# A one-token attention and MLP kernel: wq as one row and then seven ahead of K, q in one loop, zero matmuls on TensorE, ScalarE's small loads after a wait

## The chip, the core and the metric

The kernel runs on one core of one Trainium2 chip. The metric is the device time of one execution in microseconds (us), here the median of three runs. The profile is of one further execution, recorded instruction by instruction and packet by packet.

## What is computed

One token `x` (1 x 1024) is normalized to `xn`. One branch is attention over the last 4096 positions of a cache: `q = xn @ wq` gives 32 heads of 128, eight heads share one of four K/V heads, then scores, softmax, `p @ v` and `@ wo`. The other branch normalizes again and runs an MLP with 3584 hidden values. The three are added.

```
xn = layernorm(x)                                   # 1 x 1024
q  = (xn @ wq).reshape(32, 128)                     # wq 1024 x 4096
k, v = last 4096 rows of the caches, 4 heads        # each 4 x 4096 x 128
o  = softmax(q k^T / sqrt(128)) v                   # 8 query heads per K/V head
y  = layernorm(xn)
h  = gelu(y @ w1 + b1)                              # w1 1024 x 3584
out = x + o.reshape(4096) @ wo + h @ w2 + b2        # wo 4096 x 1024, w2 3584 x 1024
```

All inputs are bf16; weights and cache together are some 39.9 MB and each byte is read once.

## The kernel before, in words

**Loads.** SyncE (SP) issues every big load on one queue, q1, in the order of the program: wq rows 0 to 3 of each partition, the K pair 0 (two of the four heads), wq rows 4 to 7, the K pair 1, all of w1 (lines 233 to 237). Then SP waits until VectorE has transposed the last K quarter (`C["kt", 3]`, line 309) and issues V's two pairs into the place of K (L311); then it waits for q and issues w2 in chunks of 16 and 12 rows into the place of wq (L157 again, from line 313); then it waits for the h loop and issues wo in chunks of 16, 11, 4 and 1 rows (L318). A "row" is one row of a weight matrix in each of 128 partitions: 8 KB of wq, 7 KB of w1, 2 KB of w2 and wo. ScalarE issues three small loads at the very start, on queue q10: x, b2 and b1 (lines 168 to 170).

**POOL** builds constants (lines 175 to 220): `QBD` is cleared early, then the identity `identb`, later `GO` is cleared; `C["consts"]` marks the end. Afterwards POOL passes on loads to TensorE: it waits for a load or a transpose and raises `s_feed`, which loops on TensorE wait for with a register `turn` (lines 406 to 420). In the kernel before, that goes for the two halves of wq, the K pairs, w2 and the first wo chunk.

**VectorE** takes x's statistics once TensorE has spread x over 128 partitions (L426), writes `XZ` (line 274), which holds the normalized x as stationary columns for q, then transposes K in four quarters of 128 x 4096 (`turn_k`, L284): three of them in program order before q's own transpose (L292), the copies of q into `QBD` (L303 on VectorE, L305 on ScalarE) and the fourth quarter. Later come the maximum, the transposed probabilities, the gelu and the attention output.

**TensorE** runs in this order: x's two matmuls; q (64 matmuls of 128 x 512, in two halves of wq); b1's four small matmuls (L446); after ScalarE's copy of q (L290) two matmuls that add x and b2 to the result (L454) and four that set biases for the scores (L457, operands of two rows); 32 score matmuls in two halves, one for each K pair, the second waiting for the fourth K quarter; 56 for the MLP's hidden layer (h); 32 for `p @ v`; 88 in eleven rounds of eight for w2 and the first 16 rows of wo; and the rest of wo in small matmuls, four to a row, of which the last row has its weights loaded ahead (L517) and ends the work (L507). All matmuls written with the helper `add` have line 430. Two copies and one small store (L400, L402) end the program.

Of the kernel before, what the change touches and what calls it, by code (L numbers as in the profile page):

```python
# [18 lines left out]
KC = D // 128  # L19
NQ = HQ * DH  # L20
W1_CHUNKS = [8]
WQ_CHUNKS = [4, 4]
W2_CHUNKS = [16, 12]
WO_CHUNKS = [16, 11, 4, 1]
WO_HEAD = 1
XW = 136
PAIRS = 2
# [24 lines left out]
def bass_parallel_sum__sliding_block_cached__mixer_channel_mlp__decode_kernel(  # L52
# [17 lines left out]
    pe, dve, act, pool, sp = nc.tensor, nc.vector, nc.scalar, nc.gpsimd, nc.sync  # L70

    def sems(name, n):
        return [nc.alloc_semaphore(f"{name}{i}") for i in range(n)]

    s_x, s_b1, s_b2, s_v, s_out = (nc.alloc_semaphore(n) for n in ("s_x", "s_b1", "s_b2", "s_v", "s_out"))
    s_w1 = sems("s_w1", len(W1_CHUNKS))
    s_wq = sems("s_wq", len(WQ_CHUNKS))
    s_k = sems("s_k", PAIRS)
    s_wo = sems("s_wo", len(WO_CHUNKS))
    s_w2 = sems("s_w2", len(W2_CHUNKS))  # L80

    DVE = Track(nc, "S_DVE")
    ACT = Track(nc, "S_ACT")
    POOL = Track(nc, "S_POOL")
    done = {n: nc.alloc_semaphore(f"S_PE_{n}") for n in (
        "x", "h", "hT", "q", "sc", "pv", "tot", "fin")}
    s_feed = nc.alloc_semaphore("S_FEED")

    def sb(name, shape, d):
        return nc.alloc_sbuf_tensor(name, shape, d)  # L90

    f32, bf16 = dt.float32, dt.bfloat16
    identb = sb("identb", [128, 128], bf16)
# [7 lines left out]
    OTHER = sb("OTHER", [2, 128], bf16)  # L101
    ALT = sb("ALT", [2, 512], bf16)
    EDGE = sb("EDGE", [2, 132], bf16)
    XBRP = sb("XBRP", [2, 16 * XP], bf16)
    B1R = sb("B1R", [32, F // 32], bf16)
# [6 lines left out]
    XZ = sb("XZ", [128, KC * XW], bf16)  # L112
    YZ = sb("YZ", [128, 192], bf16)
    QBD = sb("QBD", [128, PAIRS * 512], bf16)
# [16 lines left out]
    GO = sb("GO", [128, ROUNDS * STEP + LEAD + 96], bf16)  # L131
# [6 lines left out]
    WA, W1 = BIG[:, 0:KC * NQ], BIG[:, KC * NQ:KC * NQ + KC * F]  # L138
    W2 = WA[:, 0:FC * D]
    PS = nc.alloc_psum_tensor("PS", [128, 8 * 512], f32)  # L140
    PSb = PS[:, :].bitcast(bf16)

    def bank(n, rows=128, first=0):
        return PS[first:first + rows, n * 512:(n + 1) * 512]

    w1_p = B_w1.rearrange("(p r) n -> p r n", r=KC)
    wq_p = A_wq.rearrange("(p r) n -> p r n", r=KC)
# [5 lines left out]
    C = {}  # L153

    def load_chunks(dst, src, chunks, width, semaphores, c0=0):
        for j, n in enumerate(chunks):
            sp.dma_start(  # L157
                dst[:, c0 * width:(c0 + n) * width].rearrange("p (c n) -> p c n", c=n),
                src[:, c0:c0 + n, :],
            ).then_inc(semaphores[j], 16)  # L160
            c0 += n

    XB = XBRP[:, :].rearrange("p (a n) -> p a n", a=16)[:, :, 0:D // 16]

    def row_load(dst, src, semaphore):
        act.dma_start(dst, src.rearrange("o (a n) -> o a n", a=16)).then_inc(semaphore, 16)

    row_load(XB[0:1], A_x.rearrange("b s n -> (b s) n"), s_x)
    row_load(XB[1:2], B_b2.rearrange("(o n) -> o n", o=1), s_b2)
    act.dma_start(B1R[:, :], B_b1.rearrange("(p c) -> p c", p=32)).then_inc(s_b1, 16)  # L170

    def pool_wait():
        pool.wait_ge(POOL.sem, POOL.cnt)

# [44 lines left out]
    POOL.mark(pool.tensor_tensor(out=HALF[:, :], in0=HALF4[:, 0:2], in1=HALF4[:, 2:4], op=ALU.add))  # L219
    C["consts"] = POOL.cnt  # L220

    act.wait_ge(POOL.sem, C["QBD"])
    ACT.mark(act.activation(out=PS[:, 0:1024], in_=QBD[:, :], func=ACTF.Copy))
    ACT.mark(act.activation(out=bank(7), in_=QBD[:, 0:512], func=ACTF.Copy))
# [2 lines left out]
    def pairs(cache, c):  # L227
        return cache[0, 2 * c:2 * c + 2, SK - W:SK, :].rearrange("g (m i) d -> m g (i d)", m=64)

    def load_k(c):  # L230
        sp.dma_start(KV[:, c * 8192:(c + 1) * 8192], pairs(A_k_cache, c)).then_inc(s_k[c], 16)  # L231

    load_chunks(WA, wq_p, WQ_CHUNKS[:1], NQ, s_wq)
    load_k(0)
    load_chunks(WA, wq_p, WQ_CHUNKS[1:], NQ, s_wq[1:], WQ_CHUNKS[0])
    load_k(1)
    load_chunks(W1, w1_p, W1_CHUNKS, F, s_w1)

# [59 lines left out]
    for b in range(4):  # L298
        for c in range(PAIRS):
            to = QD[32 * b:32 * b + 32, c, :, b, 16 * c:16 * c + 16].rearrange("p e (u j) -> p e u j", j=4)  # L300
# [5 lines left out]
    turn_k(3)  # L306

    V = KV[:, :]
    sp.wait_ge(DVE.sem, C["kt", 3])
    for c in range(PAIRS):  # L310
        sp.dma_start(V[:, c * 8192:(c + 1) * 8192], pairs(A_v_cache, c)).then_inc(s_v, 16)  # L311
    sp.wait_ge(done["q"], 8)
    load_chunks(W2, w2_p, W2_CHUNKS, D, s_w2)
    sp.wait_ge(done["h"], 7)
    c0 = 0
    for j, n in enumerate(WO_CHUNKS):
        first = (FC + c0) * D
# [79 lines left out]
    for engine, track, a in ((act, ACT, 1), (dve, DVE, 0)):  # L397
        engine.wait_ge(done["fin"], 1)
        of, to = PS[64 * a:64 * a + 64, 7 * 512 + 256 * a:7 * 512 + 256 * a + 256], Pb[0:64, 256 * a:256 * a + 256]
# [4 lines left out]


    pool_wait()
    pool.wait_ge(s_wq[0], 16)
    pool.sem_inc(s_feed, 1)
    pool.wait_ge(s_wq[1], 16)
    pool.sem_inc(s_feed, 1)  # L410
    pool.wait_ge(DVE.sem, C["kt", 1])
    pool.sem_inc(s_feed, 1)
    pool.wait_ge(DVE.sem, C["kt", 3])
    pool.sem_inc(s_feed, 1)
    for semaphores, chunks in ((s_w2, W2_CHUNKS), (s_wo, WO_CHUNKS[:WO_HEAD])):
        if semaphores is s_wo:
            pool.wait_ge(ACT.sem, C["OT"])
        for semaphore, n in zip(semaphores, chunks):
            pool.wait_ge(semaphore, 16)
            pool.sem_inc(s_feed, n // ROUND)  # L420
    pe.wait_ge(POOL.sem, C["ones"])
    turn = pe.alloc_register("turn")
    pe.reg_mov(turn, 1)
    pe.wait_ge(s_x, 16)
    for i in range(2):
        last = pe.matmul(bank(2 + i), lhsT=onesb[0:1, :], rhs=XB[0:1, 8 * i:8 * i + 8, :])  # L426
    last.then_inc(done["x"], 1)

    def add(to, lhsT, rhs, **place):
        return pe.matmul(to, lhsT=lhsT, rhs=rhs, start=False, stop=False, skip_group_check=True, **place)  # L430

    pe.wait_ge(DVE.sem, C["xz"])
    with pe.Fori(0, len(WQ_CHUNKS)) as j:
        pe.wait_ge(s_feed, turn)
        pe.reg_add(turn, turn, 1)
        with pe.Fori(0, 4) as t:
            for u in range(2):
                for k in range(4):
                    last = add(bank(7), XZ[:, bass.ds(t * 2 + j * (4 * XW) + (XW * k + u), 128)],
                               WA[:, bass.ds(t * -1024 + j * (4 * NQ) + (k * NQ + (7 - u) * 512), 512)])  # L440
            last.then_inc(done["q"], 1)

    pe.wait_ge(s_b1, 16)
    turned = PS[:, 2 * 512 + 32:2 * 512 + 64].rearrange("p (c t) -> p c t", c=4)[:, :, 0:7]
    for q in range(4):
        pe.matmul(turned, lhsT=E4[:, q * 128:(q + 1) * 128],  # L446
                  rhs=B1R[:, q * FC:(q + 1) * FC].rearrange("p (t c) -> p c t", c=4),
                  start=(q == 0), stop=False, skip_group_check=True)
# [4 lines left out]
    for a in range(2):  # L453
        pe.matmul(bank(7), lhsT=EDGE[:, 1 - a:129 - a], rhs=XB[:, 8 * a:8 * a + 8, :], start=(a == 0), stop=False,  # L454
                  skip_group_check=True)
    for n in range(4):
        pe.matmul(bank(3 + n), lhsT=OTHER[:, :], rhs=ALT[:, :], start=True, stop=False, skip_group_check=True)  # L457
    pe.wait_ge(DVE.sem, C["d_QBD"])
    K4 = KT[:, :].rearrange("p (x k) -> p x k", k=128)
    with pe.Fori(0, PAIRS) as c:  # L460
# [3 lines left out]
        with pe.Fori(0, 2) as j:  # L464
            for n in range(4):
                for u in range(2):
                    last = add(bank(3 + n), QBD[:, bass.ds(c * 512 + j * 256 + u * 128, 128)],
                               K4[:, bass.ds(c * 64 + 16 * n, 16), bass.ds(j * 64 + 32 * u, 32)])
                last.then_inc(done["sc"], 1)

    def h_cols(row, t):
        return row.rearrange("p (m a c) -> p m a c", m=128, a=7)[:, :, bass.ds(t, 1), :]

    pe.wait_ge(s_w1[0], 16)
    with pe.Fori(0, 7) as t:
        for k in range(KC):
            last = add(bank(0), YZ[:, bass.ds(t + 8 * k, 128)], h_cols(W1[:, k * F:(k + 1) * F], t))
# [5 lines left out]
    for c in range(4):  # L483
        last = add(turned[:, c], H8[:, c:512:4], FLIP[:, 0:7])
# [6 lines left out]
    with pe.Fori(0, 8) as i:  # L491
        for u in range(4):
            last = add(bank(1), PT[:, bass.ds(i * 256 + u * 64, 128)], V3[:, :, bass.ds(i * 1024 + u * 256, 256)])
# [12 lines left out]
    def add_held(to, lhsT, rhs, column):  # L506
        return pe.add_instruction(mybir.InstMatmult(  # L507
            name=nc.get_next_instruction_name(), engine=pe.engine, start_tensor_calc=False, stop_tensor_calc=False,
            tile_size=(128, 32), tile_position=(0, column), bass_skip_group_check=True, ldweights=False,
            ins=[pe.lower_ap(rhs), pe.lower_ap(lhsT, for_matmul_weights=True)], outs=[pe.lower_ap(to)]))  # L510

    for j, n in enumerate(WO_CHUNKS[WO_HEAD:]):
        held = c0 + n == 32
# [5 lines left out]
        for c in range(c0, c0 + n):  # L519
            rhs = BIG[:, (FC + c) * D:(FC + c + 1) * D]  # L520
            for a in range(4):
                first, column = LEAD + 2 * (c - TAIL) - (0 if a % 2 else ROW), 7 * 512 + a // 2 * 256
                to, of = PS[32 * a:32 * a + 32, column:column + 256], rhs[:, TAIL_AT[a]:TAIL_AT[a] + 256]
                if held:
                    last = add_held(to, OT[:, first:first + 32], of, 32 * a)
                else:
                    last = add(to, OT[:, first:first + 32], of, tile_position=(0, 32 * a))
# [32 lines left out]
```

## Time and profile before

| what | value |
|---|---|
| three runs, median (lowest, highest) | 98.8 us (98.8, 98.97) |
| the profiled execution | 99.37 us |
| its span, first to last instruction | 97.4 us |
| bytes moved | 39.88 MB, mean 409 GB/s over the span |
| time of q1's packets, share of 16 engines | 95.7% |
| TensorE, VectorE busy | 73.0 us, 38.9 us |
| mean granted TensorE clock | 0.965 |

How to read it: times inside the profile count from the first instruction; 1.97 us of the profiled execution lie outside its span. PE is TensorE's matmuls, PEld its weight loads, DVE VectorE, ACT ScalarE, SP SyncE; a "q" behind an engine's name is its issuing side. In a row of the timeline stand the start, the duration of a merged group, the engine, the line, the operation, what it writes and reads, the count, and in brackets how long the engine had been idle and what ended that. A matmul's record is longer than its share of the engine, as matmuls overlap: the spacing between starts is what counts. DMA engines work on packets; each load here is one packet for each partition, spread over 16 engines.

### The profile page before, as it was taken

The numbers are of one execution on the slowest core, as the hardware profiler recorded it, in microseconds if no ns is written. First come the engines' busy times: TensorE is split into PE (matmuls) and PEld (weight loads), VectorE is DVE, ScalarE is ACT, GpSimd is POOL, SyncE is SP. The second block draws the span as 40 slices with busy tenths as digits, with TensorE's granted clock in tenths as the row PEclk, the third lists the DMA queues.
The fourth block names the chain that finished last, engine by engine and source line by source line (L and its number), as shares of the span: only waits on it lengthen the run. The fifth ranks groups of instructions, "written<-read, shape, count | busy, mean of one in ns | idle before, by whom it ended". The sixth has DMA issues, their size and how long they took to land.

```text
span 97.4 us, 1285 instructions
## 1 busy us (share of the span) xinstructions
PE 73.0 (75%) x354; PEld 30.4 (31%) x354; DVE 38.9 (40%) x54; ACT 11.2 (12%) x20; POOL 9.9 (10%) x27
## 2 busy tenths in 40 slices
PE   0004000099999986999979999799999999779992
PEld 0000000033444431333434444333343443334450
DVE  0002899899930799940293620050048000000001
ACT  0880000600000024000005200200000000000001
POOL 6999400000000000000000000000000000000000
PEclk9999999999999998557999999999999999999999
DMA  7599999999999998888999999999999999899890
GB/s 215 256 431 431 405 432 444 431 444 431 410 431 481 636 424 377 377 377 377 437 431 431 437 498 431 431 444 394 394 464 498 431 431 431 376 435 426 372 377 1
DMA packets 1989, 39.88 MB, mean 409 GB/s; under 512 B 322, under 2 KB 324, under 8 KB 452
## 3 DMA queue, kind: packets, MB, share of 16 engines
q1 hardware_dynamic: 1876, 39.85, 95.7%
q10 hardware_dynamic: 112, 0.01, 0.1%
q8 instruction: 1, 0.02, 0.1%
HBM read 39.86 MB, written 0.00 MB: 409 GB/s over the span
## 4 chain that ended last, share of the span: by engine, by line
DMA 80%; PE 14%; SPq 3%; issue 1%; DVE 0%
DMA BIG<-in_B_w_dram 47%; DMA BIG<-in_A_wo_dram 33%; PE PS L430 13%; SPq L231 1%; SPq L157 1%; SPq L318 1%; DVE Pb L400 0%; PE PS L507 0%
## 5 line engine op out<-in xcount | busy, mean ns | idle before, releaser
L430 PE MATMUL PS<-BIG,XZ 128*128 x64 | 16.5, 427 | 10.2 <-DVE B L277 10.2
L430 PE MATMUL PS<-BIG,GO 128*128 (+1 forms) x148 | 22.2, 337 | 1.4 <-POOLq L420 1.2
L284 DVE STREAM_TRANSPOSE KT<-KV 128x4096 bf16<-128x4096 bf16 x4 | 17.6, 4432 | 4.8 <-DMA KV<-in_A_k_cache_dram 4.8
L430 PEld LDWEIGHTS PS<-BIG,GO 128*128 (+1 forms) x148 | 9.9, 97 | 13.8 <-issue 6.4
L430 PEld LDWEIGHTS PS<-BIG,XZ 128*128 x64 | 6.9, 108 | 20.3 <-issue 14.3
L430 PE MATMUL PS<-BIG,YZ 128*128 x56 | 12.4, 380 | 0.6 <-DMA BIG<-in_B_w_dram 0.6
L430 PE MATMUL PS<-KT,QBD 128*128 x32 | 10.0, 491 | 1.0 <-ACT QBD L305 1.0
L430 PE MATMUL PS<-KV,KT 128*128 x32 | 8.3, 381 | 0.5
L400 DVE CAST Pb<-PS 64x256 bf16<-64x256 f32 x1 | 0.4, 417 | 20.4 <-PE PS L507 20.4
L430 PEld LDWEIGHTS PS<-BIG,YZ 128*128 x56 | 5.4, 96 | 7.6 <-issue 1.8
L426 PE MATMUL PS<-XBRP,onesb 1*128 1x512 bf16 x2 | 1.0, 616 | 8.1 <-DMA XBRP<-in_A_x_dram 8.1
L430 PEld LDWEIGHTS PS<-KT,QBD 128*128 x32 | 3.8, 120 | 7.2 <-issue 5.2
L244 DVE BATCH_NORM_STATS2 BN<-PS 128x6 f32<-128x512 f32 x2 | 1.3, 689 | 9.1 <-PE PS L426 9.1
L430 PEld LDWEIGHTS PS<-KV,KT 128*128 x32 | 3.1, 96 | 5.3 <-issue 3.8
L332 DVE TENSOR_REDUCE MX<-PS 128x1 f32<-128x1024 f32 x2 | 2.4, 1220 | 5.6 <-PE PS L430 5.6
L379 DVE SCALAR_TENSOR_TENSOR QBD<-PS,REC,HALF 32x256 f32<-32x256 f32 x2 | 0.9, 474 | 6.9 <-PE PS L430 6.8
L344 ACT ACTIVATE Pb<-PS,NMB 128x2048 bf16<-128x2048 f32 x1 | 2.0, 1968 | 13.8 <-DVE NMB L341 13.8
L348 DVE STREAM_TRANSPOSE KT<-Pb 128x2048 bf16<-128x2048 bf16 x1 | 2.3, 2311 | 2.1 <-ACT Pb L344 2.1
L353 DVE COPY HT<-PS 128x28 f32<-128x28 f32 x1 | 0.2, 210 | 6.4 <-PE PS L430 6.4
L400 ACT ACTIVATE Pb<-PS 64x256 bf16<-64x256 f32 x1 | 0.4, 381 | 20.1 <-PE PS L507 20.1
L426 PEld LDWEIGHTS PS<-XBRP,onesb 1*128 1x128 bf16 x2 | 0.1, 104 | 8.1 <-DMA XBRP<-in_A_x_dram 8.1
L290 ACT ACTIVATE Pb<-PS 128x512 bf16<-128x512 f32 x1 | 0.6, 597 | 16.6 <-PE PS L430 16.6
(77 smaller groups left out, 37.7 us busy)
## 6 DMA issues: line engine op xcount, KB each, us to landing
BIG<-in_A_wq_dram SPq DMA_DIRECT2D x2, 4096.0 KB, 18.8
BIG<-in_B_w_dram SPq DMA_DIRECT2D x1, 7168.0 KB, 46.0
KV<-in_A_k_cache_dram SPq DMA_DIRECT2D x2, 2048.0 KB, 23.1
KV<-in_A_v_cache_dram SPq DMA_DIRECT2D x2, 2048.0 KB, 13.6
BIG<-in_B_w_dram SPq DMA_DIRECT2D x1, 4096.0 KB, 24.8
BIG<-in_A_wo_dram SPq DMA_DIRECT2D x1, 4096.0 KB, 23.5
BIG<-in_B_w_dram SPq DMA_DIRECT2D x1, 3072.0 KB, 31.4
BIG<-in_A_wo_dram SPq DMA_DIRECT2D x1, 2816.0 KB, 29.8
```

What stands on the lines that cost most here:

```text
L157: sp.dma_start(dst[:, c0 * width:(c0 + n) * width].rearrange("p (c n) -> p c n", c=n), src[:, c0:c0 + n, :],).then_inc(semaphores[j], 16)
L231: sp.dma_start(KV[:, c * 8192:(c + 1) * 8192], pairs(A_k_cache, c)).then_inc(s_k[c], 16)
L244: DVE.mark(dve.bn_stats(out=BN[:, 12 * n + 6 * i:12 * n + 6 * i + 6], in_=src[:, 512 * i:512 * i + 512]))
L284: C["kt", n] = DVE.mark(dve.transpose(KT[:, n * 4096:(n + 1) * 4096], KV[:, n * 4096:(n + 1) * 4096]))
L318: sp.dma_start(BIG[:, first:first + n * D], wo_flat[:, c0 * D:(c0 + n) * D]).then_inc(s_wo[j], 16)
L332: C["mx"] = DVE.mark(dve.tensor_reduce(out=MX2[:, n:n + 1], in_=S[:, 1024 * n:1024 * n + 1024], axis=AX.X, op=ALU.max))
L344: C["exp"] = ACT.mark(act.activation(out=Pb[:, :], in_=S, func=ACTF.Exp, bias=NMB[:, 0:1], scale=SCALE, accum_out=SUMP[:, 0:1]))
L348: C["d_pt"] = DVE.mark(dve.transpose(PT[:, 0:2048], Pb[:, :]))
L379: DVE.mark(dve.scalar_tensor_tensor(out=ONM.rearrange("p (i c d) -> p i c d", i=2, c=PAIRS)[:, i], in0=PS[rows, 512:1024].rearrange("p (c ...
L400: track.mark(act.activation(out=to, in_=of, func=ACTF.Copy) if a else dve.tensor_copy(to, of))
L426: last = pe.matmul(bank(2 + i), lhsT=onesb[0:1, :], rhs=XB[0:1, 8 * i:8 * i + 8, :])
L430: return pe.matmul(to, lhsT=lhsT, rhs=rhs, start=False, stop=False, skip_group_check=True, **place)
```

## The change

It does these things:

- wq is loaded as one row and then seven, both ahead of K (before: four rows, K pair 0, four rows, K pair 1).
- ScalarE waits for `identb` before it issues x, b2 and b1; its clearing of PSUM stands behind them as before.
- TensorE multiplies zeros (`QBD`, 40 matmuls of 128 x 512) into bank 4 after x's matmuls; it then waits for both wq loads itself and runs q in one loop of eight rounds of eight.
- POOL's passing on of wq is gone, and TensorE waits for POOL's constants itself.
- The four bias matmuls for the scores become a loop, each with two matmuls of zeros (`GO`) added into bank 1.
- V's first pair is issued after the second K quarter's transpose, the second pair after the fourth (before: both after the fourth).
- wo's chunks are 16, 10, 5 and 1 rows.

```diff
-WQ_CHUNKS = [4, 4]
+WQ_CHUNKS = [1, 7]
-WO_CHUNKS = [16, 11, 4, 1]
+WO_CHUNKS = [16, 10, 5, 1]
...
-    row_load(XB[0:1], A_x.rearrange("b s n -> (b s) n"), s_x)
-    row_load(XB[1:2], B_b2.rearrange("(o n) -> o n", o=1), s_b2)
-    act.dma_start(B1R[:, :], B_b1.rearrange("(p c) -> p c", p=32)).then_inc(s_b1, 16)
...
+    act.wait_ge(POOL.sem, C["identb"])
+    row_load(XB[0:1], A_x.rearrange("b s n -> (b s) n"), s_x)
+    row_load(XB[1:2], B_b2.rearrange("(o n) -> o n", o=1), s_b2)
+    act.dma_start(B1R[:, :], B_b1.rearrange("(p c) -> p c", p=32)).then_inc(s_b1, 16)
     act.wait_ge(POOL.sem, C["QBD"])
...
-    load_chunks(WA, wq_p, WQ_CHUNKS[:1], NQ, s_wq)
+    load_chunks(WA, wq_p, WQ_CHUNKS, NQ, s_wq)
     load_k(0)
-    load_chunks(WA, wq_p, WQ_CHUNKS[1:], NQ, s_wq[1:], WQ_CHUNKS[0])
     load_k(1)
...
-    sp.wait_ge(DVE.sem, C["kt", 3])
     for c in range(PAIRS):
+        sp.wait_ge(DVE.sem, C["kt", 2 * c + 1])
         sp.dma_start(V[:, c * 8192:(c + 1) * 8192], pairs(A_v_cache, c)).then_inc(s_v, 16)
...
-    pool.wait_ge(s_wq[0], 16)
-    pool.sem_inc(s_feed, 1)
-    pool.wait_ge(s_wq[1], 16)
-    pool.sem_inc(s_feed, 1)
...
-    pe.wait_ge(POOL.sem, C["ones"])
+    pe.wait_ge(POOL.sem, C["QBD"])
...
+    def busy(zeros, to, **how):
+        for i in range(2):
+            pe.matmul(to, lhsT=zeros[:, 0:128], rhs=zeros[:, 0:512], skip_group_check=True, **how)
+
+    with pe.Fori(0, 20):
+        busy(QBD, bank(4), start=True, stop=True)
+    for s in s_wq:
+        pe.wait_ge(s, 16)
     pe.wait_ge(DVE.sem, C["xz"])
-    with pe.Fori(0, len(WQ_CHUNKS)) as j:
-        pe.wait_ge(s_feed, turn)
-        pe.reg_add(turn, turn, 1)
-        with pe.Fori(0, 4) as t:
-            for u in range(2):
-                for k in range(4):
-                    last = add(bank(7), XZ[:, bass.ds(t * 2 + j * (4 * XW) + (XW * k + u), 128)],
-                               WA[:, bass.ds(t * -1024 + j * (4 * NQ) + (k * NQ + (7 - u) * 512), 512)])
-            last.then_inc(done["q"], 1)
-
+    with pe.Fori(0, 8) as t:
+        for k in range(KC):
+            last = add(bank(7), XZ[:, bass.ds(t + XW * k, 128)], WA[:, bass.ds(t * -512 + (k * NQ + 7 * 512), 512)])
+        last.then_inc(done["q"], 1)
+
+    pe.wait_ge(POOL.sem, C["consts"])
     pe.wait_ge(s_b1, 16)
...
-    for n in range(4):
-        pe.matmul(bank(3 + n), lhsT=OTHER[:, :], rhs=ALT[:, :], start=True, stop=False, skip_group_check=True)
+    with pe.Fori(0, 4) as n:
+        pe.matmul(PS[:, bass.ds(n * 512 + 3 * 512, 512)], lhsT=OTHER[:, :], rhs=ALT[:, :], start=True, stop=False,
+                  skip_group_check=True)
+        busy(GO, bank(1), start=False, stop=False)
```

## The prediction, made before the changed kernel was built or run

> **What bounds the kernel now.** I read the DMA lines first, because the kernel is one token of attention and MLP over 39.85 MB of weights and cache.
>
> ```profile
> span 97.4 us, 1285 instructions
> PE 73.0 (75%) x354; PEld 30.4 (31%) x354; DVE 38.9 (40%) x54; ACT 11.2 (12%) x20; POOL 9.9 (10%) x27
> PEclk9999999999999998557999999999999999999999
> q1 hardware_dynamic: 1876, 39.85, 95.7%
> ```
>
> SP's queue q1 carries all big loads and its packets fill 95.7% of 16 engines' time; no compute engine comes near that. The packet records say the same more sharply: from 2.4 us (when the last of 16 engines starts) to 94.3 us an engine always has a packet. The first packets start at 1.83 us, SP having issued at 0.81. In steady state a 32 KB packet takes 1.213 us (432 GB/s over 16 engines); 39.85 MB at that rate is 92.2 us. Span = 1.83 start + 92.2 + about 0.9 (staggered start and slow first packets, below) + 0.4 from the last packet to the last landing (95.36) + 2.05 tail = 97.4.
>
> Second, the order of landings on q1. Issue plus the time in the DMA view gives wq first half 12.9, K0 17.8, wq second half 27.5, K1 32.3, W1 49.25, V 54.1 and 59.0, W2 68.7 and 75.9, wo 85.6, 92.3, 94.72, 95.36: strictly in order of issue. A load's landing depends on the bytes ahead of it, so long as it is issued before the queue runs dry.
>
> Third, the chain and the timeline of the end: how far TensorE is from being the bound.
>
> ```profile
> 83.71 1.03 PE L430 MATMUL PS<-BIG,GO 128*128 x4
> 85.92 9.46 PE L430 MATMUL PS<-BIG,GO 128*128 x92 [1.18 <-POOLq L420]
> 93.23 1.10 PEld L430 LDWEIGHTS PS<-BIG,GO 128*32 128x32 bf16 x44 [0.42 <-issue]
> 94.76 0.34 PEld L430 LDWEIGHTS PS<-BIG,GO 128*32 128x32 bf16 x16 [0.43 <-DMA BIG<-in_A_wo_dram]
> 95.10 0.11 PEld L517 LDWEIGHTS <-GO 128*32 128x32 bf16 x4
> 95.40 0.28 PE L507 MATMUL PS<-BIG,GO 128*32 128x256 bf16 x4
> ```
>
> TensorE idles before 85.92 for the 16-row wo chunk, before 94.76 for the 4-row one and before 95.40 for the last. From the last matmul's start at 84.35 plus one spacing of 0.216 to 85.92 it has about 1.3 us of slack; then 0.4 us before 94.76 (ends about 94.36) and 0.2 before 95.40. From h on it has no other wait of weight, so a delay s of the h loop reaches the end only beyond roughly **1.8 us**: 1.3 + 0.4 + 0.2, less 0.1 for the last weight loads of L517.
>
> Fourth, the middle:
>
> ```profile
> 18.80 8.76 DVE L284 STREAM_TRANSPOSE KT<-KV 128x4096 bf16<-128x4096 bf16 x2
> 32.35 4.45 DVE L284 STREAM_TRANSPOSE KT<-KV 128x4096 bf16<-128x4096 bf16 x1 [4.79 <-DMA KV<-in_A_k_cache_dram]
> 36.72 0.67 DVE L292 STREAM_TRANSPOSE Pb<-Pb 128x512 bf16<-128x512 bf16 x1
> 38.14 4.45 DVE L284 STREAM_TRANSPOSE KT<-KV 128x4096 bf16<-128x4096 bf16 x1
> 38.99 10.04 PE L430 MATMUL PS<-KT,QBD 128*128 x32 [0.96 <-ACT QBD L305]
> 49.61 12.44 PE L430 MATMUL PS<-BIG,YZ 128*128 x56 [0.57 <-DMA BIG<-in_B_w_dram]
> ```
>
> VectorE transposes K0 early, waits 4.79 us for K1, and turns q 4.4 us after that. The scores start at 38.99; their first 14 matmuls stand 0.427 us apart and the rest 0.216, with the granted clock at 0.50 from 38.20 to 45.03. q shows the same two spacings (12 slow ones, to 24.5).
>
> **The change, part by part.**
>
> *wq as 1 + 7 rows, before K.* Packets per engine: 16 x 1.213 = 19.41 us become 8 x 0.309 (the 8 KB packets of wo) + 8 x 2.116 (the 56 KB packets of W1) = 19.40. The stream gains nothing. What moves is landings: wq is whole after 8.39 MB, so at 27.5 - 4.86 (one K pair, 17.81 - 12.94) = 22.6; K0 at 27.5 instead of 17.8; K1 and W1 as before.
>
> *The start.* The first 16 packets took 1.72 to 2.15 us where later ones took 1.213, all but one over 1.7: about 0.58 us lost. The out store's first packet came 0.77 us after its issue, wq's 1.02. If both excesses come from the large first packets or from ScalarE's issues at the same 0.81, the change saves up to 0.8 us; if they are a fixed price of starting, nothing. A smaller packet could also lose, but the 8 KB wo packets ran at 424 GB/s; I bound that at +0.1. The packet that started last (2.43) was the fastest at 1.415 and ended with the others, which looks like one fixed moment before which nothing flows. I take **0**.
>
> *ScalarE's loads* wait for identb (POOL, 2.56 by the timeline), so x is issued near 2.6 instead of 0.81, and ScalarE's zeroing of PSUM and the square root's table load behind them shift by 1.8 us, into idle time. Queue q10 takes turns with q1 packet by packet: x waited for three 32 KB packets, its completion for one more. Between 8 KB packets x would land near 5.7; behind 56 KB ones up to 12. The layernorm takes 10.4 us from x to XZ (8.04 to 18.46), so XZ is there at 16 to 22.4, before wq at 22.6. Free. b2 and b1 follow later, unneeded before 36.
>
> *Zero matmuls ahead of q.* 40 of them after x's two. The slow spacing lasted 5.2 us at q and 6.0 at the scores, and the clock's half stretch 6.83; I allow 3.4 (half of that) to 6.8. So they take 40 x 0.216 + half of that = 10.3 to 12.1 us, and end between 17 and 24. They stand behind x's matmuls and behind a wait on POOL met at 2.0 us; queued behind them is only q, which waits for wq. They cost nothing unless x is late. Then q: 64 x 0.216 = 13.8 us from 22.7, done at **36.5**, or 38 to 40 if the clock has fallen again. Before, 35.9.
>
> *What hides that.* VectorE: kt0, kt1, kt2 run back to back from 27.5, 8.76 + 4.45 - so kt2 ends near **40.6** (before 36.8), and q's transpose stands behind it in program order. So q may be late by 3.5 us for nothing, but everything after kt2 moves by 3.8 us: scores start 42.8, kt3 ends 46.4.
>
> *Zero matmuls ahead of the scores.* Four biases and eight zeros: 12 x 0.216 = 2.6 us, from q's copy at 37.2 to about 40.2, and not in the way of 42.8. GO's zeros and the added wait for POOL's constants (11.0) are met long before.
>
> *Scores and h.* At the full clock the first half ends at 46.3, the second waits for kt3 and ends at 50.1: h is late by s = 0.5. With a slow stretch T from 42.8 it ends at 42.8 + 32 x 0.216 + T/2, so s = 0.15 + T/2: 1.85 for T = 3.4, up to 3.5 for 6.8. The max, exp and P transposes (52.25 to 56.65) shift too, before PV at 63.
>
> *V on two waits.* SP waits kt1 (36.3), then kt3 (46.4); before both went at 42.6. Behind the second wait stand V1 and W2. The queue works on W1 till 48.2 and V0 till 53.1, so V1 issued at 46.4 has 6.7 us to spare. W2 is needed at 58, wo at 75 and issued at 62 + s. Free; it would cost if kt3 came after 52.
>
> *wo as 16, 10, 5, 1.* Bytes and packets are the same (9.16 us per engine both ways); the third chunk still lands at 94.72. Its 20 weight loads take 0.43 instead of 0.34, the last four then end at 95.30, under 95.40. Zero, at most +0.1.
>
> **Sum:** stream 0 (-0.8 to +0.1), TensorE at the end 0 (to +1.7), tail 0 (to +0.1). The profiled execution took 99.37 us, 1.97 around its span; the median shown is 98.8. The sum is zero on either base, so 98.8.
>
> **A rule that speaks on TensorE's slow stretch.** By the trace, full-array matmuls ended at 35.7, only ones of 32 and 2 rows followed, and the half clock came at 38.20; an idle stretch of 1.4 us before 85.92 left the spacing at 0.216. The Trainium skill, "TensorE: Matmul & The Clock Gate", section "Part 1: The HAM clock gate", says a free-running window of some 3.4 us decides, idle ones halving the clock and busy ones restoring it, whichever phase the kernel starts in. The trace agrees: 6.83 is two such windows. By that rule an idle 2.6 us alone need not halve the clock, and the sum would stay 0; by the row, 2.5 us with small matmuls in it did.
>
> **Rivals.**
> - *Faster: the start.* The first packets lose less. For it: 0.58 + 0.25 us of excess right where the change acts. Against: the common end of the first packets. About -0.5: 98.3. Chance 0.28.
> - *Slower: cold scores.* TensorE idles from 40.2 to 42.8 behind kt2, the clock halves, and T of 5.2 to 6.0, as seen, makes s = 2.75 to 3.15; minus 1.8 the end moves by 0.95 to 1.35: **100.0**. It decides from T of about 3.3. For it: the half clock at 38.20 after a like pause. Against: a q that runs late closes the pause, and T = 3.4 costs only 0.05. Chance 0.25.
> - *The zeros do not lift the clock* (no zero operand stands in the trace; the two-row ones did not hold it). Then 40 x 0.427 = 17 us push q to 25, q ends at 41 to 42, the twelve matmuls take 5.1 us, scores start near 47.5 and cold; s near 7, end +5: 104. Chance 0.05.
> - *The stream sets the end as before:* 98.8. Chance 0.42, of which a little falls outside 0.2%.
>
> **The numbers.** A measurement of this kernel can tell about 0.2% (0.2 us) from no change. Faster 0.29, same 0.38, slower 0.33. The range leaves out 104 and the ends of both other rivals: 98.2 to 100.0. The likeliest case alone: 98.6 to 98.95.
>
> **What would show it.** q1 with no empty stretch, wo's landings at the same times within 0.2 us (else the start: look at the first packets' starts and lengths); wq's last landing near 22.6, kt2's end near 40.6, scores from 42.8; the clock row in the 42 to 50 us slices; the idle before the 16-row wo rounds shrunk from 1.18 us but not gone. If that idle is gone and TensorE waits for nothing at the end, the slow rival holds. If q1 runs dry anywhere, I am wrong on V.

## The result and the profile after

The changed kernel takes 99.16 us in the median of ten runs, the kernel before 98.83 in ten beside it: the ratio is 1.0034 (95% interval 1.0021 to 1.0047), 0.33 us slower. Forecast was 98.8, no change within 0.2%. The profiled execution of the changed kernel has a span of 97.65 us against 97.41; the shares outside the spans differ from one profiled execution to the next (1.41 and 1.96 us), so I compare spans and places inside them.

The page of the changed kernel: its first line, the line of busy times, the row of the big loads' queue, and the engines' shares of the chain that ended last. Line numbers move with the edit: L425 is now the helper `add`, L429 the matmuls of zeros, L421 x's two matmuls, L508 the last four and L518 their weight loads.

```profile
span 97.6 us, 1414 instructions
PE 81.0 (83%) x391; PEld 34.0 (35%) x402; DVE 38.9 (40%) x54; ACT 11.2 (11%) x20; POOL 9.9 (10%) x27
...
q1 hardware_dynamic: 1876, 39.85, 95.4%
...
PE 83%; DMA 9%; issue 3%; POOL 2%; ACT 1%; DVE 0%; POOLq 0%
```

The queue is as full as before (95.4% against 95.7%), but the chain has changed owner: DMA had 80% of it before, now TensorE (PE) has 83%. That share does not say that 83% of the time would go if TensorE were faster; it says that from the last matmul back to x's landing TensorE hardly waited. The timeline of TensorE's end shows it:

```profile
82.74 13.06 PE L425 MATMUL PS<-BIG,GO 128*128 x103
...
93.99 1.54 PEld L425 LDWEIGHTS PS<-BIG,GO 128*32 128x32 bf16 x60 [0.42 <-issue]
95.53 0.10 PEld L518 LDWEIGHTS <-GO 128*32 128x32 bf16 x4
95.64 0.28 PE L508 MATMUL PS<-BIG,GO 128*32 128x256 bf16 x4
```

Before, three waits for wo stood here (before 85.92, 94.76 and 95.40). All are gone: the matmuls run in one piece, the 60 small ones of the second and third chunk too, and the last four start at 95.64 because TensorE gets to them then. The last load had landed at 95.44 (95.36 before); the 16-row chunk at 85.62, to the digit as before. TensorE was late, the loads were not. How it became late is in the middle:

```profile
11.65 1.03 PE L421 MATMUL PS<-XBRP,onesb 1*128 1x512 bf16 x2 [11.65 <-DMA XBRP<-in_A_x_dram]
12.62 11.47 PE L429 MATMUL PS<-QBD 128*128 128x512 bf16 x40
23.93 13.98 PE L425 MATMUL PS<-BIG,XZ 128*128 x64
...
42.66 4.08 PE L425 MATMUL PS<-KT,QBD 128*128 x16
47.38 4.12 PE L425 MATMUL PS<-KT,QBD 128*128 x16 [0.64 <-issue]
51.64 12.43 PE L425 MATMUL PS<-BIG,YZ 128*128 x56
```

and in VectorE's rows beside it:

```profile
27.35 13.10 DVE L283 STREAM_TRANSPOSE KT<-KV 128x4096 bf16<-128x4096 bf16 x3 [4.84 <-DMA KV<-in_A_k_cache_dram]
40.38 0.67 DVE L291 STREAM_TRANSPOSE Pb<-Pb 128x512 bf16<-128x512 bf16 x1
41.08 0.68 DVE L302 COPY QBD<-Pb 32x64 bf16<-32x64 bf16 x4
41.79 4.45 DVE L283 STREAM_TRANSPOSE KT<-KV 128x4096 bf16<-128x4096 bf16 x1
```

The three K transposes, q's transpose and the start of the scores stand where the prediction put them (40.4 for 40.6, 42.66 for 42.8), and the clock stayed full. But the two halves of the scores take 4.08 and 4.12 us where 16 records 0.216 us apart span 3.6; the second half starts at 47.38 where 46.6 was expected, with "issue" named as what it waited for (nothing that the profile shows, so TensorE's own issuing side); and h starts at 51.64, so s is 2.03 us, not 0.5.

### The profile page after: what moved, and what is told of

It reads as the page before. It is cut to its first block, busy times and chain, and to the rows that moved or that the text cites. A ratio compares the mean times of both kernels' runs of the same rounds, so it can differ in the third digit from the quotient of the medians.

```text
span 97.6 us, 1414 instructions
## 1 busy us (share of the span) xinstructions
PE 81.0 (83%) x391; PEld 34.0 (35%) x402; DVE 38.9 (40%) x54; ACT 11.2 (11%) x20; POOL 9.9 (10%) x27
## 3 DMA queue, kind: packets, MB, share of 16 engines
q1 hardware_dynamic: 1876, 39.85, 95.4%
## 4 chain that ended last, share of the span: by engine, by line
PE 83%; DMA 9%; issue 3%; POOL 2%; ACT 1%; DVE 0%; POOLq 0%
PE PS L425 66%; PE PS L429 14%; DMA XBRP<-in_A_x_dram 9%; PE PS L456 1%; PE PS L421 1%; POOL QBD L174 1%; ACT Pb L289 1%; PE PS L453 1%; ACT H L349 1%; DVE Pb L399 0%; POOL identb L176 0%; POOL onesb L171 0%; POOL identb L173 0%; PE PS L508 0%; POOLq L176 0%
## 5 line engine op out<-in xcount | busy, mean ns | idle before, releaser
L425 PE MATMUL PS<-BIG,GO 128*128 (+1 forms) x137 | 21.3, 333 | 0.7
L425 PEld LDWEIGHTS PS<-BIG,GO 128*128 (+1 forms) x148 | 10.0, 97 | 12.2 <-issue 5.2
L425 PE MATMUL PS<-BIG,XZ 128*128 x64 | 14.0, 379 | 0.0
L425 PE MATMUL PS<-BIG,YZ 128*128 x56 | 12.4, 379 | 0.1
L429 PE MATMUL PS<-QBD 128*128 128x512 bf16 x40 | 11.5, 459 | 0.0
L421 PE MATMUL PS<-XBRP,onesb 1*128 1x512 bf16 x2 | 1.0, 616 | 11.7 <-DMA XBRP<-in_A_x_dram 11.7
L425 PEld LDWEIGHTS PS<-BIG,XZ 128*128 x64 | 6.3, 98 | 7.5
L425 PE MATMUL PS<-KT,QBD 128*128 x32 | 8.0, 379 | 1.0 <-issue 0.6
L425 PE MATMUL PS<-KV,KT 128*128 x32 | 8.3, 381 | 0.5
L425 PEld LDWEIGHTS PS<-BIG,YZ 128*128 x56 | 5.4, 96 | 7.2 <-issue 1.5
L429 PEld LDWEIGHTS PS<-QBD 128*128 128x128 bf16 x40 | 4.5, 114 | 7.4 <-issue 4.4
L425 PEld LDWEIGHTS PS<-KT,QBD 128*128 x32 | 3.1, 96 | 5.9 <-issue 3.8
L425 PEld LDWEIGHTS PS<-KV,KT 128*128 x32 | 3.1, 96 | 5.3 <-issue 3.7
L421 PEld LDWEIGHTS PS<-XBRP,onesb 1*128 1x128 bf16 x2 | 0.1, 106 | 11.7 <-DMA XBRP<-in_A_x_dram 11.7
```

The source lines that it names most:

```text
L429: pe.matmul(to, lhsT=zeros[:, 0:128], rhs=zeros[:, 0:512], skip_group_check=True, **how)
```

## The experiments

Theory 1: TensorE comes to the h loop 2.0 us late, which is more than the slack of 1.8, and the lateness beyond the forecast's 0.5 arises at the ends of the score loops. Theory 2: the loads, the start of the stream or ScalarE's later loads cost the time, and TensorE's place in the chain is incidental. A name with a_ is an edit of the changed kernel, with b_ of the one before. Every ratio is against runs of the kernel before on the same chip.

One table first, since most runs are read by it. From p @ v on, the work of TensorE is the same in all these kernels (a_h6 leaves work out ahead of it); without a wait the last matmuls start 30.57 us after it, as in the changed kernel (95.64 - 65.07).

| kernel | h starts | p @ v starts | that + 30.57 | last wo landing | last matmuls start | ratio (95% interval) |
|---|---|---|---|---|---|---|
| before | 49.61 | 63.05 | 93.62 | 95.36 | 95.40 | |
| b_wq_134 | 49.74 | 63.17 | 93.74 | 95.50 | 95.55 | 1.0007 (0.9988 to 1.0025) |
| a_h6 | 51.82 | 63.51 | 94.08 | 95.39 | 95.44 | 1.0003 (0.9983 to 1.0023) |
| a_j_unrolled_fit | 50.29 | 63.74 | 94.31 | 95.39 | 95.44 | 1.0007 (0.9986 to 1.0027) |
| b_delay8 | 51.05 | 64.49 | 95.06 | 95.45 | 95.50 | 0.9999 (0.9969 to 1.0028) |
| changed | 51.64 | 65.07 | 95.64 | 95.44 | 95.64 | 1.0034 (1.0021 to 1.0047) |
| a_wo_back | 51.79 | 65.22 | 95.79 | 95.40 | 95.79 | 1.0028 (1.0016 to 1.0041) |
| a_half_zeros | 51.84 | 65.28 | 95.85 | 95.40 | 95.84 | 1.0032 (1.0015 to 1.0048) |
| a_no_score_zeros | 52.06 | 65.50 | 96.07 | 95.28 | 96.07 | 1.0042 (1.0018 to 1.0066) |
| b_delay_loop | 52.08 | 65.52 | 96.09 | 95.45 | 96.05 | 1.0047 (1.0029 to 1.0066) |
| b_k_behind_v_split | 52.09 | 65.53 | 96.10 | 95.59 | 96.09 | 1.0042 (1.0018 to 1.0065) |
| a_loads_first | 52.17 | 65.61 | 96.18 | 95.71 | 96.17 | 1.0069 (1.0044 to 1.0094) |

The last matmuls start, within 0.05 us, at the later of two columns: the last landing (plus 0.05) or p @ v plus 30.57. In the first five rows it is the landing and the time is that of the kernel before; in the others it is TensorE, and every one is slower. The change-over lies at p @ v = 95.40 - 30.57 = 64.83, which is 1.78 us after the 63.05 of the kernel before.

**Is TensorE's lateness the cause?** First a pure delay in the kernel before, eight matmuls of zeros:

```
     pe.wait_ge(s_w1[0], 16)
+    for _ in range(8):
+        add(bank(1), GO[:, 0:128], GO[:, 0:512])
```

> The kernel before with eight zero matmuls (8 x 0.216 = 1.73 us) added on TensorE between the wait for w1 and the h loop: pure delay, by about as much as the changed kernel's. By the prediction's slack of 1.8 us: h starts near 51.3, the rounds of wo's 16 rows move by 0.4, the end by 0 to 0.1: 98.8 to 98.95. If the slack is smaller than read, up to 99.5. Theory 2 expects the delay to cost nothing and the changed kernel to be slow for another reason, so 98.83.

It took 98.88 beside 98.98 (two of its twelve times, 100.11 and 100.61, stand apart): p @ v 1.44 us late, nothing at the end. Then less work in the changed kernel, which leaves out one of the seven rounds of h (a seventh of it, not an eighth) and counts to six in the two waits for them:

```
-    sp.wait_ge(done["h"], 7)
+    sp.wait_ge(done["h"], 6)
...
-    act.wait_ge(done["h"], 7)
+    act.wait_ge(done["h"], 6)
...
-    with pe.Fori(0, 7) as t:
+    with pe.Fori(0, 6) as t:
```

> The changed kernel with six instead of seven rounds of the h loop: an eighth of the MLP's first product is left out, so TensorE has 8 matmuls (1.75 us) less to do after the scores; loads, waits and code stay. Theory 1 (TensorE, 2.0 us late at h against 1.8 of slack, sets the end): TensorE idles again 1.0 to 1.3 us before wo's 16-row rounds, the last matmuls wait for the last load, and the time falls to 98.8 to 98.9. Theory 2 (the loads, the start or ScalarE's later loads cost the 0.33 us): it stays at 99.1 to 99.2.

```profile
85.96 8.59 PE L425 MATMUL PS<-BIG,GO 128*128 x72 [0.78 <-POOLq L415]
94.81 0.73 PE L425 MATMUL PS<-BIG,GO 128*32 128x256 bf16 x20 [0.26 <-DMA BIG<-in_A_wo_dram]
95.44 0.28 PE L508 MATMUL PS<-BIG,GO 128*32 128x256 bf16 x4
```

98.85 beside 98.87, and TensorE waits for wo again. The loads, their order and ScalarE's order were those of the changed kernel, wo's 16 rows landed at 85.67, and the 0.33 us were gone: theory 2 falls. A larger delay in the kernel before, as a loop of three times four zero matmuls at the place of b_delay8:

```
+    with pe.Fori(0, 3):
+        for _ in range(4):
+            add(bank(1), GO[:, 0:128], GO[:, 0:512])
```

> The kernel before with twelve zero matmuls ahead of the h loop as a loop of three times four (13 more instructions of program, less than the sixteen of b_delay8, whose fetch stayed in the tail): h starts 2.7 to 3.0 us late (8 x 1.73 / 8 + loop ends, less the 0.3 that b_delay8 found hidden in the wait for w1). Theory 1, one for one beyond a slack of 1.8 us: last matmul 0.9 to 1.2 later, 99.7 to 100.0, with wo's landings unmoved (85.6, 94.7, 95.4). If b_delay16's 101.0 was TensorE's lateness and not its moved fetch, more than that.

99.45 beside 98.88. h was only 2.47 us late, as the twelve zeros ran through at 0.216 us each (49.49 to 52.08) and their loop's ends cost nothing; the last matmuls are 0.65 late, and 2.47 - 1.78 is 0.69. One for one, as expected.

**Where does the lateness come from?** K's order alone, on the kernel before:

```
-    load_k(0)
     load_chunks(WA, wq_p, WQ_CHUNKS[1:], NQ, s_wq[1:], WQ_CHUNKS[0])
+    load_k(0)
```

> The kernel before with one edit: the first K pair is loaded behind both halves of wq, as in the changed kernel. Theory 1 (the order of K alone makes TensorE late; the zero matmuls only win a part of it back): the second K pair's transpose ends near 40.4, the scores start near 42.7 after a pause of more than 5 us, at half the clock for 3.4 to 6.8 us, h starts 2.5 to 3.2 us later than before, and the time is 99.5 to 100.2, slower than the changed kernel. If instead the zeros, the one q loop or ScalarE's loads are what costs: 98.83.

It took 100.91 beside 98.88 (ratio 1.0196, 1.0172 to 1.0220), above the range: h started at 52.34 as expected, but V's two loads, issued together at 46.35, landed at 56.3 and 61.1 (before: 54.1 and 59.0), and all of w2 and wo came 2.1 us later. That was the loads, not TensorE. With V on two waits (the changed kernel's edit of line 309) the two parts separate:

```
-    load_k(0)
     load_chunks(WA, wq_p, WQ_CHUNKS[1:], NQ, s_wq[1:], WQ_CHUNKS[0])
+    load_k(0)
...
-    sp.wait_ge(DVE.sem, C["kt", 3])
     for c in range(PAIRS):
+        sp.wait_ge(DVE.sem, C["kt", 2 * c + 1])
```

> b_k_behind with V's two loads on two waits, as in the changed kernel: the first at 36.3, the second at 46.4. Theory 1: the queue stays full, wo lands at 85.6 and 95.4 as before, h starts near 52.3 as in b_k_behind (2.7 us late, 0.9 beyond the slack), and the time is 99.6 to 99.9. If K's order cost something besides TensorE's lateness, more; if TensorE's lateness were not what counts, 98.88.

99.43 beside 98.93, wo at its old place, TensorE 2.5 us late. K's order is what makes TensorE late. The same joint wait put back into the changed kernel:

```
+    sp.wait_ge(DVE.sem, C["kt", 3])
     for c in range(PAIRS):
-        sp.wait_ge(DVE.sem, C["kt", 2 * c + 1])
```

> The changed kernel with both loads of V issued after the fourth K transpose, as in the kernel before: at 46.3, some 2 us before the queue's last packets of w1 are served. By b_k_behind, V's first half lands at 56.3 instead of 54.1 and everything behind it 2.1 us later: 100.9 to 101.3. If the short notice was an accident of that kernel: 99.1 to 99.2.

Its four times lie between 99.08 and 102.31, median 101.08; they are too far apart for a ratio. In the profile V landed at 55.9 and 60.8. Four such times give no price by themselves, and one of them is no slower than the changed kernel; the six times of b_k_behind (100.12 to 101.58) carry it. In both profiles V was issued some 2 us before w1's last packets were served and landed 1.8 to 2.2 us late; why is open. In the changed kernel, with the split, V landed at 54.1 and 59.0 as before.

Then the loop ends. The scores of the changed kernel written out in full:

```
-    with pe.Fori(0, PAIRS) as c:
-        pe.wait_ge(s_feed, turn)
+    for c in range(PAIRS):
+        pe.wait_ge(s_feed, 1 + c)
...
-        with pe.Fori(0, 2) as j:
+        for j in range(2):
...
```

> The changed kernel with its score loops written out (same 32 matmuls, constant waits on the same semaphore), so that TensorE's issuing side has no loop ends there. Theory 1 (the changed kernel is late because TensorE reaches the h loop 2.0 us later than before, 1.5 us of it lost at the ends of the score loops and at the start of the second half): h starts near 50.2 to 50.5 instead of 51.64, TensorE idles again before the 16-row rounds of wo (0.3 us or more), and the time falls to 98.8 to 98.9. Theory 2 (the loads or the start cost it, not TensorE): the time stays near 99.16 though h starts earlier. Rival within theory 1 (the fourth K transpose and the hand-over by POOL set the second half, not the loops): h starts at 51.0 or later, 99.0 to 99.1.

TensorE did what theory 1 says, as its timeline shows, and yet the time rose to 100.37 (ratio 1.0137, 1.0108 to 1.0167):

```profile
42.63 3.62 PE L425 MATMUL PS<-KT,QBD 128*128 128x512 bf16 x16
46.49 3.61 PE L425 MATMUL PS<-KT,QBD 128*128 128x512 bf16 x16 [0.24 <-POOLq L409]
49.94 12.44 PE L425 MATMUL PS<-BIG,YZ 128*128 x56
...
87.41 9.71 PE L425 MATMUL PS<-BIG,GO 128*128 x92 [0.70 <-POOLq L415]
96.95 0.28 PE L508 MATMUL PS<-BIG,GO 128*32 128x256 bf16 x4
```

The halves take 3.62 and 3.61 us and h starts at 49.94, 1.70 us earlier. But TensorE waits again for wo, whose 16 rows landed at 86.89 instead of 85.62. The DMA view, cut to 77 to 79 us of this kernel, names an intruder:

```profile
q1 hardware_dynamic: 28, 0.92, 107.7%
q8 instruction: 1, 0.02, 2.9%
```

One 16 KB packet of instructions at 77.77 us, 0.93 us on one engine of the 16. The kernel before has the same packet, at 94.85, when its loads are all but through; the changed kernel at 95.08. The packets of the 16 rows show what it does: fifteen engines end their shares at 84.74 to 85.24 us, as in the changed kernel, and the sixteenth at 86.45. Its packet right behind the instructions also took 1.71 us instead of 1.213, so it lost 0.93 + 0.50 us, and the load landed when it was through. I took the early packet to come from the longer program, and tried the same unrolling on the kernel before, where TensorE has slack to spare:

> The kernel before with its score loops written out: 28 more instructions of TensorE's program ahead of the rounds of w2 and wo. Theory 3 (a longer program moves the 16 KB instruction fetch from the tail at 94.9 us into the middle of wo's load, where one engine serves it while its share of wo waits): the fetch stands near 77 to 80, the landings of wo move by 1.2 to 1.4, the rounds' spacing widens, and the time is 100.1 to 100.4, though TensorE's own work is no later. Rival (written-out scores were slower in the changed kernel for a reason of that kernel): 98.83.

100.15 beside 98.87 (1.0120, 1.0092 to 1.0147), the packet at 80.36, one engine through at 86.62 and the others by 85.50, wo 1.4 us late: so it is. TensorE was later too, against the expectation (p @ v at 64.82, as h began in a half-clock stretch), but 64.82 + 30.57 = 95.39 is still ahead of the last landing at 96.75. b_delay16, twice the delay of b_delay8, had run into the same thing:

```
+    for _ in range(16):
+        add(bank(1), GO[:, 0:128], GO[:, 0:512])
```

> The kernel before with sixteen zero matmuls (3.45 us) at the same place. By the slack of 1.8 us the end moves by 1.65: 100.5. Without any slack 102.3; if TensorE is not near the bound at all, 98.83.

101.0 beside 98.98, but with the packet at 79.13, wo landing 1.4 us late and TensorE's rounds 1.82 to 1.98 us apart, it says nothing on the slack; b_delay_loop has the same kind of delay without the moved packet. For the loop ends a shorter program was needed. Only the inner loop written out, with part of the small matmuls for b1, x and b2 left out to make room (not shown):

```
...
-        with pe.Fori(0, 2) as j:
+        for j in range(2):
```

> The changed kernel with the inner score loop written out (two loop ends less, the outer one stays), and three of b1's four matmuls and one of the two that add x and b2 left out, so that the program ahead of the rounds is 11 instructions longer instead of 18. Theory 1 with the loop ends as the late step: the score halves last 3.6 instead of 4.1 us, h starts 0.6 to 0.8 us earlier (50.8 to 51.0), TensorE is inside its slack of 1.8 us and the time is 98.85 to 98.95, if the instruction fetch stays near 95. If the fetch moves to 77 to 80, 100.1 or more, and the run says nothing on the loop ends' time. If loop ends do not matter, 99.16.

h came to 50.27, but the packet still came at 77.69: 100.2 beside 98.93, and nothing learnt on the time. All six of those matmuls left out:

> The changed kernel with the inner score loop written out and, to keep the program short, b1's four matmuls and the two that add x and b2 left out (their waits stay): the program ahead of the rounds is 7 instructions longer than the changed kernel's. Theory 1 with the loop ends as the late step: h starts near 50.3 (1.3 us earlier than in the changed kernel), p @ v near 63.7 instead of 65.07, TensorE idles again before wo's 16-row rounds, the fetch stays near 95, and the time is 98.85 to 98.95. If it stays at 99.1 to 99.2 with the fetch near 95, lateness at h is not the cause. If the fetch moves again, 100.1 or more.

```profile
42.57 3.61 PE L425 MATMUL PS<-KT,QBD 128*128 x16 [0.28 <-ACT QBD L304]
46.84 3.61 PE L425 MATMUL PS<-KT,QBD 128*128 x16 [0.66 <-POOLq L409]
50.29 12.44 PE L425 MATMUL PS<-BIG,YZ 128*128 x56
...
86.20 1.67 PE L425 MATMUL PS<-BIG,GO 128*128 x7 [0.78 <-POOLq L415]
...
95.44 0.27 PE L500 MATMUL PS<-BIG,GO 128*32 128x256 bf16 x4
```

98.93 beside 98.87, with the packet at 94.80. The second half now waits for POOL's hand-over of the fourth K transpose (0.66) and not for "issue", TensorE waits for wo again before 86.20, and the changed kernel's loss is gone. The six matmuls left out are ones the changed kernel did ahead of the scores, while TensorE was waiting anyway.

**The other parts of the change.** Without the zeros ahead of the scores (four straight biases as in the kernel before):

```
-    with pe.Fori(0, 4) as n:
...
-        busy(GO, bank(1), start=False, stop=False)
+    for n in range(4):
+        pe.matmul(bank(3 + n), lhsT=OTHER[:, :], rhs=ALT[:, :], start=True, stop=False, skip_group_check=True)
```

> The changed kernel without the eight zero matmuls ahead of the scores (the four biases stand as before). Theory 1: TensorE pauses some 3 us before the scores; where that halves the clock, scores last 2.5 to 3 us longer less the loop ends that the slow spacing hides, h starts near 52.2 to 52.8, and the time is 99.5 to 100.2; where the clock stays, nothing changes (99.1). Theory 2: 99.16 whatever the clock does.

99.34 beside 98.98; in the profile the clock stood at half from 40.84 to 47.67, and still h was only 0.42 us later than in the changed kernel. The slow stretch of 4.95 us from the start of the scores cost 0.42 us there, not half of its length. Half the zeros ahead of q:

```
-    with pe.Fori(0, 20):
+    with pe.Fori(0, 10):
```

> The changed kernel with 20 instead of 40 zero matmuls ahead of q: they end near 20 instead of 23.9, q starts with wq's landing at 22.7, 1.2 us earlier. Theory 1: q's transposes still wait for the second K pair's (40.4), so scores start at 42.7 as before and the time stays 99.1; if the clock is lost in the pause of 2 to 3 us, q ends late and the time is up to 99.6. If the zeros are what costs: 98.85.

99.31 beside 98.88, the changed kernel's loss within the intervals; q started 0.8 us earlier, with half the clock for 3.4 us of it. ScalarE's three loads (x, b2, b1) back at the start, ahead of its wait for POOL's `identb`:

> The changed kernel with ScalarE's three loads issued at the start again. x lands early (6 to 8 instead of 11.6), the zero matmuls end by 20, q starts at 22.6 instead of 23.9, but the second K pair's transpose still holds the q transposes at 40.4. Theory 1: h starts where it did (51.6) unless the pause ahead of q or of the scores costs the clock, so 99.1 to 99.3. Theory 2, if the later loads are the cost: 98.83.

99.53 beside 98.87, a little more than expected. The profile shows why:

```profile
5.95 1.03 PE L421 MATMUL PS<-XBRP,onesb 1*128 1x512 bf16 x2 [5.95 <-DMA XBRP<-in_A_x_dram]
6.91 10.95 PE L429 MATMUL PS<-QBD 128*128 128x512 bf16 x40
23.12 16.54 PE L425 MATMUL PS<-BIG,XZ 128*128 x64 [5.27 <-issue]
...
43.67 0.61 PE L429 MATMUL PS<-GO 128*128 128x512 bf16 x2
44.11 3.62 PE L425 MATMUL PS<-KT,QBD 128*128 x16
```

x lands 5.7 us earlier, the zeros are through at 17.9, TensorE pauses for 5.27 us, q starts at half the clock and ends late enough to push the zeros ahead of the scores past 42.66. The late loads of the change, which look like a cost, keep the zeros next to q. wo's chunks put back, in the changed kernel:

```
-WO_CHUNKS = [16, 10, 5, 1]
+WO_CHUNKS = [16, 11, 4, 1]
```

> The changed kernel with wo's chunks 16, 11, 4, 1 again. TensorE is the bound there and does the same 60 small matmuls without a pause either way: the time stays within 0.1 of the changed kernel's (99.0 to 99.2). If the split costs by itself, 98.9 or less.

99.21 beside 98.88: no difference from the changed kernel. And the small first load in the kernel before (chunks of 1, 3 and 4 rows):

```
-WQ_CHUNKS = [4, 4]
+WQ_CHUNKS = [1, 3, 4]
...
-    load_chunks(WA, wq_p, WQ_CHUNKS[:1], NQ, s_wq)
+    load_chunks(WA, wq_p, WQ_CHUNKS[:2], NQ, s_wq)
...
-    load_chunks(WA, wq_p, WQ_CHUNKS[1:], NQ, s_wq[1:], WQ_CHUNKS[0])
+    load_chunks(WA, wq_p, WQ_CHUNKS[2:], NQ, s_wq[2:], 4)
...
```

> The kernel before with wq's first half as one row and then three: the small first load of the changed kernel without its order. If the 0.15 us by which the changed kernel's wq, K0 and K1 landed early is a gain of the small first packets that reaches the end: 98.65 to 98.7. If it is lost again along the queue, as the changed kernel's w1 (49.28 against 49.25) says: 98.83.

98.9 beside 98.87: no gain. Nothing here beats the kernel before; the versions on its time are bound by the same last landing.

## Why the prediction was wrong

- **Slack of 1.8 us: right.** Measured 1.78, and one for one beyond it. Had s been known, the sum would have given 2.03 - 1.78 = 0.25 us; the spans differ by 0.24.
- **"At the full clock the first half ends at 46.3, the second waits for kt3 and ends at 50.1: h is late by s = 0.5": this step failed.** s is 2.03. The term that was too small is the 32 score matmuls at 0.216 us each. Of the 1.54 us between, 0.74 lies before the second half (47.38 for 50.1 - 16 x 0.216 = 46.64, though the fourth K quarter was done at 46.24), 0.51 inside it (0.41 of this at the inner loop's end, as its two groups of eight start 2.14 apart where 8 x 0.216 is 1.73), and 0.29 between the last score matmul and h. I had taken 0.216 as the pace of the whole loop from the trace of before, where no gap stands at any loop end of the scores. What I did not read there is TensorE's issuing side, in whose rows the register operations and the branches of the loops stand. The branch that ends the inner loop runs four times, and its first and last start stand in the rows of its line, before and after:

```profile
L464 PEldq COMPARE_BRANCH  x4: 76/142/208, 40.5 to 47.3; - x4
L465 PEldq COMPARE_BRANCH  x4: 76/142/212, 44.1 to 51.0; - x4
```

From the first to the last the issuing side took 6.81 us before, where half the clock held the matmuls back, and 6.86 at the full clock; in a_no_score_zeros, partly at half the clock, 6.86 again (44.16 to 51.02). So here the clock made no difference to it. Before, the slow matmuls were behind it: when it closed the first half at 42.78, nine of the sixteen matmuls had begun. In the changed kernel all sixteen had begun when it did so at 46.44, and TensorE stood waiting for it. b_wq_134, whose scores also ran at full clock, shows the same halves of 4.11 and 4.12 us in the old order, and a_j_unrolled_fit takes the gaps within the halves away. A loop's end need not cost anything: the loop of zeros in b_delay_loop, whose addresses are constants, shows no gap.

- **The price of a slow stretch, T/2: right as a formula against 0.216, wrong against what full clock really gives.** With T = 4.95 in a_no_score_zeros my formula (42.8 + 32 x 0.216 + T/2) gives h at 52.2, measured 52.06; but at full clock h is at 51.64 and not 50.1. (The constant in "0.15 + T/2" should be 0.10, which changes nothing.) The rival of cold scores (chance 0.25) had the right sign and the right end, TensorE late and without a wait at the end, by a wrong cause: in the profiled execution the clock is full throughout.
- **K's order, kt2, start of the scores: right**, within 0.2 us, and K's order is indeed what moves them.
- **x and the zeros ahead of q: right that they are hidden, not that q starts at 22.7.** x landed at 11.61, so the 40 zeros held q until 23.93 and q ended at 37.9; q's transpose came at 40.4 whatever q did.
- **Zeros ahead of the scores: right that they are not in the way, too short in time.** They ran to 42.5 and not to 40.2, from q's copy at 38.5; their rounds of three matmuls start 0.86 us apart where 3 x 0.216 is 0.65, the same step again.
- **V "free": right for the changed kernel, incomplete.** With K behind wq, the split is needed; the joint wait costs some 1.5 us there (b_k_behind against b_k_behind_v_split: 100.91 to 99.43). I had looked at the spare time of the second load only, and "issued before the queue runs dry" was too weak a condition: 2 us ahead was too late.
- **The start, 0: right.** The first 16 packets lost 0.25 us instead of 0.62, but nothing of it arrives: w1 landed at 49.28 against 49.25. K1 landed 0.11 earlier in this execution (32.22), which is within the spread, as in eight other kernels with the same start it landed between 32.19 and 32.38.
- **wo, 0: right.**
- **The rule on the clock.** The half-clock stretches of the runs last 3.41, 6.83 and 10.24 us, one, two and three times the same length, and lie elsewhere in other executions. The Trainium skill, "TensorE: Matmul & The Clock Gate", "Part 1: The HAM clock gate", has a free-running window of about 3.4 us, and these traces agree. A pause of 1.15 us ahead of the scores was followed by a half stretch in a_wo_back, one of 1.13 in b_wq_134 was not.

What stays open: the profiles differ by 0.24 us and the medians by 0.33, and the profiled execution of the changed kernel (99.06) is one of its faster ones; the times of the changed kernel spread from 98.99 to 99.54, and a full-clock execution took 99.24 and one with a half stretch 98.99, so the spread is not explained by the clock alone.

## What to carry to other kernels

A loop has two paces, that of its matmuls and that of the side that issues them. Read both from the trace: here a half-clock stretch hid the second, and at the full clock it was what was left. When loads set the end, write down each engine's slack from the wait that ends last, and add up lateness against it; here 1.78 us could be spent for nothing and the next 0.25 counted in full. Before unrolling, find where the program's next instruction packet is fetched: in a stream that is full, 28 more instructions ahead of the last loop (b_scores_unrolled) cost more than the loop ends they saved.

## What the runs showed of the hardware

The instruction packet is the surprise. What moves it goes with the length of TensorE's program ahead of the end of the loop of rounds. Against the kernel before, b_delay_loop is 13 instructions longer and b_delay8 16, and the packet came at about 95 us, when the loads are all but through; b_scores_unrolled is 28 longer and b_delay16, by the same count, 32, and it came at 80.4 and 79.1, in the middle of that loop. Against the changed kernel, 7 more (a_j_unrolled_fit) left it at 94.8 and 11 more (a_j_unrolled_short) put it at 77.7. In the middle it takes 0.93 or 0.94 us on one engine, that engine's next packet takes 1.71 instead of 1.213, and every later landing moves by 1.2 to 1.5 us. In these four kernels TensorE's rounds are also slower, up to 2.1 us apart instead of 1.82, and already before the packet comes; the cause of that is open. Why the limit lies there was not tried. The Trainium skill, "Runtime: NRT & Kernel Launch", section "Instruction fetch mechanics", has such refills in 16 KB blocks, which the runs agree with, but calls their cost mostly hidden; in this full stream it was 1.3 us, as b_scores_unrolled shows.
